# Five wider tiles of u, and weights made as (1 + fraction) times a power of two, in an attention and gated-FFN kernel that TensorE bounds

## The chip, the cores and the metric

The kernel runs on one core of one Trainium2 chip. The metric is the device time of one execution in microseconds (us). The engines are called PE (TensorE), DVE (VectorE), ACT (ScalarE), POOL (GpSimd) and SP (SyncE, which here issues transfers). All runs that are compared were in the fast state, at a mean granted PE clock of 0.997 to 1.0; a kernel that ran only once in a batch carries no state ("unknown"), and is used for its trace (and, for the changed kernel, as one of its 13 starts below). "Span" is the time from the first to the last instruction; the device time is 2.1 to 2.6 us longer. In the lines of the profile, PEld is the weight loads of PE, SPq the issuing of transfers, "L397" line 397 of the kernel, "at<-kv,qT" what is written and what is read, x12 a count, and a bracket at the end the idle time before the line and what ended it. Edits move the line numbers: the matmuls of the plain blocks are L397 in the kernel before, L400 in the changed one, L403 with the tiles alone and L394 with the conversion alone.

## The reference

Per batch and head (8 x 8, 576 tokens, 64 columns): `kv = k^T v`, `u = q kv`, and `x = u / rms(u) * g`. Then `out = (sigmoid(x Wg) * (x Wv)) Wo` on 4608 tokens, with 512 model columns and 1536 hidden columns.

```python
kv = np.einsum('bhsd,bhse->bhde', k, v)
out = np.einsum('bhsd,bhde->bhse', q, kv)
rms = np.sqrt(np.mean(out * out, axis=-1, keepdims=True) + 1e-06)
x = out / rms * g_norm
gate = 1.0 / (1.0 + np.exp(-(x @ w_gate)))
return gate * (x @ w_val) @ w_out
```

The three weights lie in HBM as 64-bit floats. The kernel has no such type, so it reads each as two 32-bit words and makes the 32-bit float by integer and float operations on 1024 columns a partition: one such group is a "unit", and there are 18 of them.

## The kernel before

Two heads are one "pair"; there are 32. The first eight go through a start of their own, in stages of several pairs at once; the other 24 are fed, piece by piece, between the matmuls of the FFN. u of a pair is made in six matmuls of 96 tokens:

```python
def u_mm():
    ps = at_ps("u")
    d["u"] = ps[0:NP, :, 0:JH * P]                    # NP = 96 tokens, P = 128 columns
    for j in range(NJ):                               # NJ = 6
        nc.tensor.matmul(ps[0:NP, j // JH, c0:c0 + P], d["qT"][...96 columns...], kvs[n % 2], ...)
```

The conversion of a unit is seven DVE steps (s0 to s6), and an Abs on ACT. The steps are handed out a few at a time, in the stages of the start and in the blocks of the first FFN layer ("plain" blocks, 16 matmul passes or 6.87 us of PE each):

```python
for i in range(NE + 1):                               # NE = 8 pairs
    stage(i, 3 if i < 2 else 1 if i == 2 else 0)      # second argument: conversion steps
    ...
blk = Plain(0, 0, ...)                                # block 0, chunk 0, weights of unit 0
for m in range(NMT): blk.mm(0, m)
do(NE - 1, U_SUM, U_ROOT)
take_abs(1)
do(NE - 2, X, X_OUT)
do(NE - 1, U_NORM)
convert_some(2)
... two matmuls, do(NE - 1, X, X_OUT), two matmuls ...
convert_some(2)
blk.gate()                                            # sigmoid on ACT
blk.end()                                             # gate product on DVE
blocks = [(1, 0)] + [(c, f) for f in range(1, NFT - 3) for c in range(2)] + ...
```

So unit 1 is first wanted by the third block, (0, 1).

Of the kernel before, what the change touches and what calls it, by code (L numbers as in the profile page):

```python
# [3 lines left out]

# [5 lines left out]

FP32 = mybir.dt.float32
U32 = mybir.dt.uint32
I64 = mybir.dt.int64
AF = mybir.ActivationFunctionType
ALU = mybir.AluOpType
AX = mybir.AxisListType


HI_MIN = struct.unpack("<f", struct.pack("<I", 0x38100000))[0]
HI_MAX = struct.unpack("<f", struct.pack("<I", 0x47EFFFFF))[0]  # L20


@with_exitstack
def kernel(
# [11 lines left out]
    nc = tc.nc  # L36

    B, H, S, HD = q.shape
    T, DM = out.shape
    DF = moe_w_gate.shape[1]  # L40
    P = 128
    NHP = H // 2
    NJ = 6
    NP = S // NJ
    JH = NJ // 2
    NMT = DM // P
    NFT = DF // P
    G = 512
# [41 lines left out]
    units = [("gv", f) for f in range(NFT)] + [("wo", f) for f in range(0, NFT, 2)]  # L90
    UW = 2 * NMT * P
    assert NMT * P == DM
    staged, absolute, w = {}, {}, {}

    def load_unit(u):
        if u >= len(units):
# [13 lines left out]
    def words(u):  # L110
        t = staged[u].rearrange("p i f -> p (i f)").bitcast(U32).rearrange("p (n two) -> p n two", two=2)
        return t[:, :, 0], t[:, :, 1]

    def take_abs(u):
        if u >= len(units):
            return
        absolute[u] = z = raw.tile([P, UW], U32, tag="cz", name="cz", bufs=2)
        nc.scalar.activation(out=z.bitcast(FP32), in_=words(u)[1].bitcast(FP32), func=AF.Abs)

    def convert(u):  # L120
        kind, f = units[u]
        vec = nc.vector
        d = {}

        def fl(t):
            return t.bitcast(FP32)

        def s0():

            t = const.tile([P, 2, DM], FP32, name=f"{kind}{f}") if kind == "gv" else w2[:, f:f + 2, :]  # L130
            if kind == "gv":
                for i, name in enumerate(("wg", "wv")):
                    w[name, f] = t[:, i].rearrange("p (m f) -> p m f", m=NMT)
            else:
                for i in range(2):
                    w["wo", f + i] = t[:, i]
            d["x"] = t.rearrange("p i f -> p (i f)").bitcast(U32)
            vec.tensor_scalar(out=fl(d["x"]), in0=fl(words(u)[1]), scalar1=HI_MAX, scalar2=-HI_MAX,
                              op0=ALU.min, op1=ALU.max)

        def s1():

            x, z = d["x"], absolute[u]
            vec.scalar_tensor_tensor(out=fl(x), in0=fl(z), scalar=HI_MIN, in1=fl(x), op0=ALU.is_ge, op1=ALU.mult)

        def s2():
            if u:
                take_abs(u + 1)

            vec.tensor_scalar(out=absolute[u], in0=d["x"], scalar1=0x07FFFFFF, scalar2=3, op0=ALU.bitwise_and,  # L150
                              op1=ALU.logical_shift_left)

        def s3():
            x, z = d["x"], absolute[u]
            vec.scalar_tensor_tensor(out=x, in0=x, scalar=0xC0000000, in1=z, op0=ALU.bitwise_and, op1=ALU.bitwise_or)

        def s4():

            vec.tensor_scalar(out=absolute[u], in0=d["x"], scalar1=0xFF800000, scalar2=None, op0=ALU.bitwise_and)

        def s5():
            z = absolute[u]
            vec.scalar_tensor_tensor(out=fl(z), in0=words(u)[0], scalar=2.0 ** -52, in1=fl(z),
                                     op0=ALU.mult, op1=ALU.mult)

        def s6():
            x, z = d["x"], absolute[u]
            vec.tensor_tensor(out=fl(x), in0=fl(z), in1=fl(x), op=ALU.add)
            if u:
                load_next_unit()  # L170

        return [s0, s1, s2, s3, s4, s5, s6]

    converts = deque(s for u in range(len(units)) for s in convert(u))
    made = [0]

    def convert_some(n):
        for _ in range(min(n, len(converts))):
            converts.popleft()()
            made[0] += 1  # L180

    def converted(u):
        convert_some(7 * (u + 1) - made[0])

    for n in range(4):
        load_kv(n)
# [26 lines left out]
    def attention(n, at_ps):  # L213

        b, m = divmod(n, NHP)
        d = {}

        def kv_mm():
            d["kv"] = ps = at_ps("kv")
            for j in range(NJ):  # L220
                js = slice(HD * j, HD * j + HD)
                for e in range(2):
                    nc.tensor.matmul(ps[HD * e:HD * e + HD, 0, 0:HD], pairs[n]["k"][:, e, js], pairs[n]["v"][:, e, js],  # L223
                                     start=(j == 0), stop=(j == NJ - 1))

        def kv_out():
            for e in range(2):
                es = slice(HD * e, HD * e + HD)
                nc.vector.tensor_copy(out=kvs[n % 2][es, es], in_=d["kv"][es, 0, 0:HD])
            for i in ahead(n, 2):  # L230
                load_kv(i)

        def q_mm():
            d["q"] = ps = at_ps("q")
            for j in range(NJ):
                c0 = NP * (j % JH)
                nc.tensor.transpose(ps[:, j // JH, c0:c0 + NP], pairs[n]["q"][:, j].rearrange("p e d -> p (e d)"),  # L237
                                    ident[0:NP, 0:NP])

        def q_out():  # L240
            d["qT"] = sb.tile([P, 2, JH * NP], FP32, tag="qT", name="qT")
            nc.scalar.copy(out=d["qT"], in_=d["q"][:, :, 0:JH * NP])
            for i in ahead(n, 1):
                load_q(i)

        def u_mm():

            ps = at_ps("u")
            d["u"] = ps[0:NP, :, 0:JH * P]
            for j in range(NJ):  # L250
                c0 = P * (j % JH)
                nc.tensor.matmul(ps[0:NP, j // JH, c0:c0 + P], d["qT"][:, j // JH, NP * (j % JH):NP * (j % JH) + NP],  # L252
                                 kvs[n % 2], start=True, stop=True)

        def u_square():
            d["sq"] = sb.tile([NP, 2, JH * P], FP32, tag="sq", name="sq")
            nc.scalar.activation(out=d["sq"], in_=d["u"], func=AF.Square)

        def u_sum():
            d["ms"] = sb.tile([NP, 2, 2 * JH], FP32, tag="ms", name="ms")  # L260
            nc.vector.tensor_reduce(out=d["ms"].rearrange("p i n -> p (i n)"),  # L261
                                    in_=d["sq"].rearrange("p i (n d) -> p (i n) d", d=HD), axis=AX.X, op=ALU.add)

        def u_root():
            nc.scalar.activation(out=d["ms"], in_=d["ms"], func=AF.Sqrt, bias=eps[0:NP], scale=1.0 / HD)

        def u_norm():
            nc.vector.reciprocal(d["ms"], d["ms"])
            d["xn"] = d["sq"]
            nc.vector.tensor_tensor(out=d["xn"].rearrange("p i (n d) -> p i n d", d=HD),  # L270
                                    in0=d["u"].rearrange("p i (n d) -> p i n d", d=HD),
                                    in1=d["ms"].unsqueeze(3).to_broadcast([NP, 2, 2 * JH, HD]), op=ALU.mult)

        def x_mm():
            d["x"] = ps = at_ps("x")
            for j in range(NJ):
                c0 = NP * (j % JH)
                nc.tensor.transpose(ps[:, j // JH, c0:c0 + NP], d["xn"][:, j // JH, P * (j % JH):P * (j % JH) + P],  # L278
                                    ident[0:NP, 0:NP])

        def x_out():

            s0 = 0
            while s0 < S:
                c, o = divmod(S * b + s0, G)
                i, r = divmod(s0, S // 2)
                n_ = min(G - o, S // 2 - r)
                nc.scalar.activation(out=chunk(c)[:, m, o:o + n_], in_=d["x"][:, i, r:r + n_], func=AF.Copy, scale=g_col)
                s0 += n_

        return [kv_mm, kv_out, q_mm, q_out, u_mm, u_square, u_sum, u_root, u_norm, x_mm, x_out]


# [119 lines left out]
    def halves(t):  # L413
        return t[:, 0], t[:, 1]
# [23 lines left out]
    def stage(i, n_convert):  # L438
        do(i, KV, Q, KV_OUT, Q_OUT)
        do(i - 2, U_SUM, U_ROOT, U_NORM)  # L440
        do(i - 1, U, U_SQUARE)
        do(i - 3, X, X_OUT)
        if i == 0:
            take_abs(0)
        convert_some(n_convert)

    for i in range(NE + 1):
        stage(i, 3 if i < 2 else 1 if i == 2 else 0)
        if i + 5 == NE:
            load_next_unit()  # L450
            load_next_unit()
# [1 line left out]
    for m in range(NMT):  # L453
        blk.mm(0, m)
    do(NE - 1, U_SUM, U_ROOT)
    take_abs(1)
    do(NE - 2, X, X_OUT)
    do(NE - 1, U_NORM)
    convert_some(2)
# [9 lines left out]
    blk.end()  # L469
    blocks = [(1, 0)] + [(c, f) for f in range(1, NFT - 3) for c in range(2)] + [(0, f) for f in range(NFT - 3, NFT)]  # L470
    for n, (c, f) in enumerate(blocks):
        plain(c, f, 7 if n == 0 else 6, halves(two(n % 4)))
    assert n % 4 == 3
    finish()
    convert_some(len(converts))
# [223 lines left out]
```

## Time and profile before

| before | us |
|---|---|
| device time, median of the first 3 runs | 1135.58 (1133.63 to 1135.91) |
| span of the profiled run | 1133.9 |
| PE busy | 1113.2 |
| first matmul of the first block | 45.82 |
| last matmul over | 1130.02 |
| rest (last sum, last store) | 3.88 |

The prediction shows the lines that carry this. For the argument, the span is cut in three: the **start**, up to the first matmul of the first block; the **stretch**, from there to the end of the last matmul, in which PE is fed almost without a gap; and the **rest**, after it. The stretch is 1130.02 - 45.82 = 1084.20 us.

### The profile page before, as it was taken

The page shows a single profiled execution, that of the slowest core. Times are in us where ns is not written, and L with a number is a line of the kernel's source. Part 1 is how long each engine was busy: PE and PEld are TensorE (multiplying, and loading weights), DVE is VectorE, ACT ScalarE, POOL GpSimd, SP SyncE. Part 2 cuts the span into 40 slices and gives each one's busy share as a digit, 9 for nine tenths or more (in the row PEclk, how much of TensorE's full clock was granted, in tenths as well). Part 3 has the DMA queues.
Part 4 walks back from the last instruction along what each step waited for, and adds up shares of the span by engine and source line. Part 5 has one row for each costly group of instructions (what it writes and reads, how often), then busy time and mean ns, then how long its engine had stood idle before and what let it go on. Part 6 is the DMA issues. An engine that isn't in the chain of part 4 may idle for free.

```text
span 1133.9 us, 14824 instructions
## 1 busy us (share of the span) xinstructions
PE 1113.2 (98%) x5712; PEld 892.0 (79%) x5712; DVE 582.1 (51%) x1121; ACT 296.9 (26%) x571; POOL 239.5 (21%) x342
## 2 busy tenths in 40 slices
PE   5899999999999999999999999999999999999998
PEld 5644444547888888888888888888888888888887
DVE  4699996054155624563365415552556246615641
ACT  3622221223033303331243213340333112101110
POOL 0000001000033303430133104330333035404420
PEclk9999999999999999999999999999999999999999
DMA  9943431220312012110202030201100000000001
GB/s 221 231 137 123 149 111 33 49 71 11 78 23 53 11 26 64 40 35 20 71 11 54 20 75 16 53 11 38 53 11 11 20 19 1 1 21 17 1 1 38
DMA packets 71589, 57.58 MB, mean 51 GB/s; under 512 B 40800, under 2 KB 65376, under 8 KB 71520
## 3 DMA queue, kind: packets, MB, share of 16 engines
q1 hardware_dynamic: 71360, 56.64, 19.3%
q8 instruction: 46, 0.75, 0.3%
q14 instruction: 23, 0.19, 0.1%
q10 hardware_dynamic: 160, 0.00, 0.0%
HBM read 47.19 MB, written 9.44 MB: 50 GB/s over the span
## 4 chain that ended last, share of the span: by engine, by line
PE 94%; DMA 3%; DVE 2%; SPq 0%; issue 0%; ACT 0%; DVEq 0%
PE mm L526 45%; PE mm L606 26%; PE two L397 10%; PE mm L382 4%; PE at L397 3%; DMA q<-in_q_dram 3%; PE at L252 3%; PE at L223 2%; PE at L278 1%; PE at L237 1%; PE mm L397 1%; DVE sq L270 0%; DVE ms L261 0%; SPq L85 0%; SPq L76 0%; DVE w L648 0%
## 5 line engine op out<-in xcount | busy, mean ns | idle before, releaser
L512 POOL TENSOR_TENSOR tw<-gv 128x256 f32<-128x256 f32 x168 | 120.4, 727 | 843.5 <-PE mm L526 653.7
L526 PE MATMUL mm<-xT,tw 128*128 128x256 f32 x672 | 159.7, 380 | 0.0
L526 PE MATMUL mm<-sx,tw 128*128 128x256 f32 x672 | 159.7, 380 | 0.0
L526 PE MATMUL mm<-xT,gv 128*128 128x256 f32 x672 | 158.8, 379 | 0.0
L526 PEld LDWEIGHTS mm<-xT,gv 128*128 128x128 f32 x672 | 127.7, 190 | 17.4
L526 PEld LDWEIGHTS mm<-sx,tw 128*128 128x128 f32 x672 | 126.1, 190 | 16.7
L526 PEld LDWEIGHTS mm<-xT,tw 128*128 128x128 f32 x672 | 125.3, 190 | 16.1
L512 POOL TENSOR_TENSOR tw<-gv,tw 128x256 f32<-128x256 f32 x168 | 123.6, 757 | 0.0
L397 PE MATMUL two<-xT,gv 128*128 128x512 f32 x256 | 111.1, 593 | 0.5 <-DVE sq L270 0.5
L397 PEld LDWEIGHTS two<-xT,gv 128*128 128x128 f32 x256 | 48.4, 190 | 60.4 <-issue 60.2
L606 PE MATMUL mm<-t2w,gv 128*128 128x256 f32 x384 | 89.1, 379 | 0.0
L606 PE MATMUL mm<-w,gv 128*128 128x256 f32 x384 | 88.1, 379 | 0.0
L606 PE MATMUL mm<-w,s 128*128 128x256 f32 x384 | 88.1, 379 | 0.0
L555 ACT ACTIVATE sg<-sg 128x256 f32<-128x256 f32 x84 | 35.0, 417 | 190.2 <-DVE sg L554 188.9
L546 DVE TENSOR_TENSOR gv<-mm,sg 128x256 f32<-128x256 f32 x84 | 35.7, 425 | 88.5 <-PE mm L526 88.5
L606 PEld LDWEIGHTS mm<-w,s 128*128 128x128 f32 x384 | 73.0, 190 | 9.9
L606 PEld LDWEIGHTS mm<-t2w,gv 128*128 128x128 f32 x384 | 72.6, 190 | 9.7
L606 PEld LDWEIGHTS mm<-w,gv 128*128 128x128 f32 x384 | 72.5, 190 | 9.6
L526 PE MATMUL mm<-sx,gv 128*128 128x256 f32 x336 | 79.5, 379 | 0.0
L526 PEld LDWEIGHTS mm<-sx,gv 128*128 128x128 f32 x336 | 63.1, 190 | 8.2
L533 ACT COPY sg<-mm 128x256 f32<-128x256 f32 x84 | 31.3, 373 | 140.6 <-PE mm L526 140.4
L562 DVE TENSOR_TENSOR gv<-gv,sg 128x512 f32<-128x512 f32 x84 | 67.1, 838 | 0.2
(94 smaller groups left out, 1191.1 us busy)
## 6 DMA issues: line engine op xcount, KB each, us to landing
k<-in_k_dram SPq DMA_DIRECT2D x32, 288.0 KB, 4.8
v<-in_v_dram SPq DMA_DIRECT2D x32, 288.0 KB, 5.3
q<-in_q_dram SPq DMA_DIRECT2D x64, 144.0 KB, 3.2
st<-in_moe_w_gate_dram SPq DMA_DIRECT2D x12, 512.0 KB, 3.7
st<-in_moe_w_val_dram SPq DMA_DIRECT2D x12, 512.0 KB, 4.7
st<-in_moe_w_out_dram SPq DMA_DIRECT2D x12, 512.0 KB, 4.4
out_dram<-sg SPq DMA_DIRECT2D x24, 192.0 KB, 2.2
out_dram<-sg SPq DMA_DIRECT2D x24, 128.0 KB, 2.3
```

The lines of the kernel that those rows point to most:

```text
L223: nc.tensor.matmul(ps[HD * e:HD * e + HD, 0, 0:HD], pairs[n]["k"][:, e, js], pairs[n]["v"][:, e, js], start=(j == 0), stop=(j == NJ - 1))
L237: nc.tensor.transpose(ps[:, j // JH, c0:c0 + NP], pairs[n]["q"][:, j].rearrange("p e d -> p (e d)"), ident[0:NP, 0:NP])
L252: nc.tensor.matmul(ps[0:NP, j // JH, c0:c0 + P], d["qT"][:, j // JH, NP * (j % JH):NP * (j % JH) + NP], kvs[n % 2], start=True, stop=True)
L382: nc.tensor.matmul(ps, gv[c, f][:, P * t:P * t + P], w["wo", f], start=(f == 0), stop=(f == NFT - 1))
L397: nc.tensor.matmul(self.ps[i], w[("wg", "wv")[i], self.f][:, m, :], xT[self.c][:, m, :], start=(m == 0), stop=(m == NMT - 1), skip_group_c ...
L512: nc.gpsimd.tensor_tensor(out=tw[f, i], in0=b[in0], in1=b[in1] if isinstance(in1, tuple) else tw[f, in1], op=ALU.subtract)
L526: nc.tensor.matmul(ps, wt[:, m, :], xs[:, m, :], start=(new and m == 0), stop=(m == NK - 1), skip_group_check=True)
L533: nc.scalar.copy(out=d["sg"][:, h2], in_=pa)
L546: tt(out=d["h"][:, h2], in0=pb, in1=d["sg"][:, h2], op=ALU.add)
L555: nc.scalar.activation(out=d["sg"][:, h2], in_=d["sg"][:, h2], func=AF.Sigmoid)
L562: tt(out=d["h"], in0=d["h"], in1=d["sg"], op=ALU.mult)
L606: nc.tensor.matmul(ps, hs(f), ws[:, f, :], start=(new and f == 0), stop=(f == NF2 - 1), skip_group_check=True)
```

## The change

Its intent: fewer passes on PE for u, and less DVE work for the weights. u gets five tiles of 115 tokens, each read as 116 rows. A weight is made as m = 1 + fraction (mask on DVE, scale and add on ACT), a power of two p (shift on DVE, integer arithmetic on ACT), then low word, sign and product in three two-source steps on DVE. The first two steps of a unit run one unit ahead, so that ACT has time.

```diff
+    NU = 5
+    M = S // NU
+    MU = S - M * (NU - 1)
+    UC = 192
...  (u_mm)
-            for j in range(NJ):
-                nc.tensor.matmul(ps[0:NP, ...], d["qT"][...], kvs[n % 2], start=True, stop=True)
+            for i in range(NU):
+                nc.tensor.matmul(d["u"][:, i], qT[:, M * i:M * i + MU], kvs[n % 2], start=True, stop=True)
...  (square, sum, normalisation: 96 x 768 becomes 116 x 640; transposes of x: five of 115 or 116)
...  (convert: the seven steps become five)
+            vec.tensor_scalar(out=m.bitcast(U32), in0=words(u)[1], scalar1=0x000FFFFF, ..., op0=ALU.bitwise_and)
+            nc.scalar.activation(out=m, in_=m.bitcast(U32), func=AF.Identity, scale=2.0 ** -20, bias=one)
+            vec.tensor_scalar(out=p, in0=words(u)[1], scalar1=20, scalar2=0x7FF, ...)
+            nc.scalar.activation(out=p.bitcast(I32), in_=p, func=AF.Relu, scale=2.0 ** 23, bias=exp_off)
+            vec.scalar_tensor_tensor(out=m, in0=words(u)[0], scalar=2.0 ** -52, in1=m, op0=ALU.mult, op1=ALU.add)
+            vec.scalar_tensor_tensor(out=p, in0=words(u)[1], scalar=0x80000000, in1=p, ...)
+            vec.tensor_tensor(out=m, in0=m, in1=d["p"].bitcast(FP32), op=ALU.mult)
...
+    converts.extend(halves_of[0][0] + halves_of[0][1] + halves_of[1][0])
+    last[0] = 5
+    for u in range(1, len(units)):
+        if u + 1 < len(units):
+            converts.extend(halves_of[u + 1][0])
+        converts.extend(halves_of[u][1])
+        last[u] = len(converts)
...
-        stage(i, 3 if i < 2 else 1 if i == 2 else 0)
+        stage(i, 2 if i < 2 else 1 if i == 2 else 0)
...
-        plain(c, f, 7 if n == 0 else 6, halves(two(n % 4)))
+        plain(c, f, 5, halves(two(n % 4)))
```

More of the change, by code (lines that the diff above doesn't have):

```diff
@@ L1 @@
-import struct
 from collections import deque
@@ L12 @@
 U32 = mybir.dt.uint32
+I32 = mybir.dt.int32
 I64 = mybir.dt.int64
@@ L16 @@
 AX = mybir.AxisListType
-HI_MIN = struct.unpack("<f", struct.pack("<I", 0x38100000))[0]
-HI_MAX = struct.unpack("<f", struct.pack("<I", 0x47EFFFFF))[0]
 @with_exitstack
@@ L45 @@
     JH = NJ // 2
+    NU = 5
+    M = S // NU
+    MU = S - M * (NU - 1)
+    UC = 192
+    UX = M * 3
     NMT = DM // P
@@ L92 @@
     assert NMT * P == DM
-    staged, absolute, w = {}, {}, {}
+    staged, w = {}, {}
     def load_unit(u):
@@ L112, in words @@
         return t[:, :, 0], t[:, :, 1]
-    def take_abs(u):
-        if u >= len(units):
-            return
-        absolute[u] = z = raw.tile([P, UW], U32, tag="cz", name="cz", bufs=2)
-        nc.scalar.activation(out=z.bitcast(FP32), in_=words(u)[1].bitcast(FP32), func=AF.Abs)
+    EXP_OFF = 896
+    one = const.tile([P, 1], FP32, name="one")
+    nc.vector.memset(one, 1.0)
+    exp_off = const.tile([P, 1], FP32, name="exp_off")
+    nc.vector.memset(exp_off, -EXP_OFF * 2.0 ** 23)
     def convert(u):
@@ L123, in convert @@
         d = {}
-        def fl(t):
-            return t.bitcast(FP32)
         def s0():
@@ L136, in s0 @@
                     w["wo", f + i] = t[:, i]
-            d["x"] = t.rearrange("p i f -> p (i f)").bitcast(U32)
-            vec.tensor_scalar(out=fl(d["x"]), in0=fl(words(u)[1]), scalar1=HI_MAX, scalar2=-HI_MAX,
-                              op0=ALU.min, op1=ALU.max)
+            d["m"] = m = t.rearrange("p i f -> p (i f)")
+            vec.tensor_scalar(out=m.bitcast(U32), in0=words(u)[1], scalar1=0x000FFFFF, scalar2=None,
+                              op0=ALU.bitwise_and)
+            nc.scalar.activation(out=m, in_=m.bitcast(U32), func=AF.Identity, scale=2.0 ** -20, bias=one)
@@ L141, in s1 @@
         def s1():
-            x, z = d["x"], absolute[u]
-            vec.scalar_tensor_tensor(out=fl(x), in0=fl(z), scalar=HI_MIN, in1=fl(x), op0=ALU.is_ge, op1=ALU.mult)
+            d["p"] = p = raw.tile([P, UW], U32, tag="cz", name="cz", bufs=2)
+            vec.tensor_scalar(out=p, in0=words(u)[1], scalar1=20, scalar2=0x7FF, op0=ALU.logical_shift_right,
+                              op1=ALU.bitwise_and)
+            nc.scalar.activation(out=p.bitcast(I32), in_=p, func=AF.Relu, scale=2.0 ** 23, bias=exp_off)
@@ L146, in s2 @@
         def s2():
-            if u:
-                take_abs(u + 1)
-            vec.tensor_scalar(out=absolute[u], in0=d["x"], scalar1=0x07FFFFFF, scalar2=3, op0=ALU.bitwise_and,
-                              op1=ALU.logical_shift_left)
+            m = d["m"]
+            vec.scalar_tensor_tensor(out=m, in0=words(u)[0], scalar=2.0 ** -52, in1=m, op0=ALU.mult, op1=ALU.add)
         def s3():
-            x, z = d["x"], absolute[u]
-            vec.scalar_tensor_tensor(out=x, in0=x, scalar=0xC0000000, in1=z, op0=ALU.bitwise_and, op1=ALU.bitwise_or)
+            p = d["p"]
@@ L157, in s4 @@
+            vec.scalar_tensor_tensor(out=p, in0=words(u)[1], scalar=0x80000000, in1=p, op0=ALU.bitwise_and,
+                                     op1=ALU.bitwise_or)
         def s4():
-            vec.tensor_scalar(out=absolute[u], in0=d["x"], scalar1=0xFF800000, scalar2=None, op0=ALU.bitwise_and)
-        def s5():
-            z = absolute[u]
-            vec.scalar_tensor_tensor(out=fl(z), in0=words(u)[0], scalar=2.0 ** -52, in1=fl(z),
-                                     op0=ALU.mult, op1=ALU.mult)
@@ L166, in s6 @@
-        def s6():
-            x, z = d["x"], absolute[u]
-            vec.tensor_tensor(out=fl(x), in0=fl(z), in1=fl(x), op=ALU.add)
+            m = d["m"]
+            vec.tensor_tensor(out=m, in0=m, in1=d["p"].bitcast(FP32), op=ALU.mult)
             if u:
                 load_next_unit()
-        return [s0, s1, s2, s3, s4, s5, s6]
-    converts = deque(s for u in range(len(units)) for s in convert(u))
+        return [s0, s1], [s2, s3, s4]
+    halves_of = [convert(u) for u in range(len(units))]
@@ L175 @@
+    converts, last = deque(), {}
+    converts.extend(halves_of[0][0] + halves_of[0][1] + halves_of[1][0])
[5 more added lines that the diff above has]
+        last[u] = len(converts)
     made = [0]
@@ L182, in converted @@
     def converted(u):
-        convert_some(7 * (u + 1) - made[0])
+        convert_some(last[u] - made[0])
     for n in range(4):
@@ L248, in u_mm @@
             ps = at_ps("u")
-            d["u"] = ps[0:NP, :, 0:JH * P]
-            for j in range(NJ):
-                c0 = P * (j % JH)
-                nc.tensor.matmul(ps[0:NP, j // JH, c0:c0 + P], d["qT"][:, j // JH, NP * (j % JH):NP * (j % JH) + NP],
-                                 kvs[n % 2], start=True, stop=True)
+            d["u"] = ps[0:MU].rearrange("p i c -> p (i c)")[:, 0:NU * UC].rearrange("p (i c) -> p i c", c=UC)[:, :, 0:P]
+            qT = d["qT"].rearrange("p i n -> p (i n)")
+            for i in range(NU):
+                nc.tensor.matmul(d["u"][:, i], qT[:, M * i:M * i + MU], kvs[n % 2], start=True, stop=True)
         def u_square():
-            d["sq"] = sb.tile([NP, 2, JH * P], FP32, tag="sq", name="sq")
+            d["sq"] = sb.tile([MU, NU, P], FP32, tag="sq", name="sq")
             nc.scalar.activation(out=d["sq"], in_=d["u"], func=AF.Square)
         def u_sum():
-            d["ms"] = sb.tile([NP, 2, 2 * JH], FP32, tag="ms", name="ms")
-            nc.vector.tensor_reduce(out=d["ms"].rearrange("p i n -> p (i n)"),
-                                    in_=d["sq"].rearrange("p i (n d) -> p (i n) d", d=HD), axis=AX.X, op=ALU.add)
+            d["ms"] = sb.tile([MU, NU, 2], FP32, tag="ms", name="ms")
+            nc.vector.tensor_reduce(out=d["ms"].rearrange("p i e -> p (i e)"),
+                                    in_=d["sq"].rearrange("p i (e d) -> p (i e) d", d=HD), axis=AX.X, op=ALU.add)
         def u_root():
-            nc.scalar.activation(out=d["ms"], in_=d["ms"], func=AF.Sqrt, bias=eps[0:NP], scale=1.0 / HD)
+            nc.scalar.activation(out=d["ms"], in_=d["ms"], func=AF.Sqrt, bias=eps[0:MU], scale=1.0 / HD)
         def u_norm():
@@ L269, in u_norm @@
             d["xn"] = d["sq"]
-            nc.vector.tensor_tensor(out=d["xn"].rearrange("p i (n d) -> p i n d", d=HD),
-                                    in0=d["u"].rearrange("p i (n d) -> p i n d", d=HD),
-                                    in1=d["ms"].unsqueeze(3).to_broadcast([NP, 2, 2 * JH, HD]), op=ALU.mult)
+            nc.vector.tensor_tensor(out=d["xn"].rearrange("p i (e d) -> p i e d", d=HD),
+                                    in0=d["u"].rearrange("p i (e d) -> p i e d", d=HD),
+                                    in1=d["ms"].unsqueeze(3).to_broadcast([MU, NU, 2, HD]), op=ALU.mult)
         def x_mm():
             d["x"] = ps = at_ps("x")
-            for j in range(NJ):
-                c0 = NP * (j % JH)
-                nc.tensor.transpose(ps[:, j // JH, c0:c0 + NP], d["xn"][:, j // JH, P * (j % JH):P * (j % JH) + P],
-                                    ident[0:NP, 0:NP])
+            for i in range(NU):
+                m_ = MU if i == NU - 1 else M
+                bank, c0 = divmod(M * i, UX)
+                nc.tensor.transpose(ps[:, bank, c0:c0 + m_], d["xn"][0:m_, i, :], ident[0:m_, 0:m_])
         def x_out():
@@ L285, in x_out @@
                 c, o = divmod(S * b + s0, G)
-                i, r = divmod(s0, S // 2)
-                n_ = min(G - o, S // 2 - r)
+                i, r = divmod(s0, UX)
+                n_ = min(G - o, (UX if i == 0 else S - UX) - r)
                 nc.scalar.activation(out=chunk(c)[:, m, o:o + n_], in_=d["x"][:, i, r:r + n_], func=AF.Copy, scale=g_col)
@@ L442, in stage @@
         do(i - 3, X, X_OUT)
-        if i == 0:
-            take_abs(0)
         convert_some(n_convert)
     for i in range(NE + 1):
-        stage(i, 3 if i < 2 else 1 if i == 2 else 0)
+        stage(i, 2 if i < 2 else 1 if i == 2 else 0)
         if i + 5 == NE:
@@ L455 @@
     do(NE - 1, U_SUM, U_ROOT)
-    take_abs(1)
     do(NE - 2, X, X_OUT)
```

## The prediction

> **What bounds the kernel now.** I read the page's busy shares and chain first, then the chain in order of time, then the timelines of the two places where TensorE (PE) is not the releaser.
>
> ```profile
> PE 1113.2 (98%) x5712; PEld 892.0 (79%) x5712; DVE 582.1 (51%) x1121; ACT 296.9 (26%) x571; POOL 239.5 (21%) x342
> ...
> PE 94%; DMA 3%; DVE 2%; SPq 0%; issue 0%; ACT 0%; DVEq 0%
> ```
>
> PE is busy 98% of the span and is 94% of the chain that ended last; VectorE (DVE), which the change mostly relieves, is busy for half of the span and is 2% of the chain. A busy share alone proves little, so I looked at what the PE waits for, in the list of waits cut to PE. After the first attention pairs it has one wait in the rest of the run, 1.3 us for a DVE normalisation; before that, waits for data and for the same DVE line:
>
> ```profile
> PE at L278 <- DVE sq L270: 1.3, 1, 1.3
> PE two L397 <- DVE sq L270: 0.5, 1, 0.5
> ```
>
> The window from 60 to 192 us, where all weights are converted on a DVE that is over 90% busy, has no PE wait at all. So four stretches count: a start of about 39.3 us that is paced by transfers (the chain there is one q load after another, 8.28, 8.27, 8.73 and 7.56 us long), a latency chain from 39.4 to 45.8 us, a PE that streams from 45.8 us to the end, and the one wait at 254.6 us. The chain in order of time, in the second stretch, with its start and its length:
>
> ```profile
> 40.62 0.96 DVE ms L261
> ...
> 41.61 0.32 ACT ms L265
> ...
> 42.20 0.95 DVE sq L270
> 43.16 0.87 DVE ms L261
> ...
> 44.72 0.97 DVE sq L270
> 45.68 0.14 issue
> 45.82 3.67 PE two L397 x8
> ...
> 52.23 22.34 PE two L397 x52
> ```
>
> Here the reader is to see that two sums (L261) and two normalisations (L270) of DVE lie on the path, and that from 45.82 us on matmuls follow each other. In the streaming stretch the u product of one pair (L252) sits between others; the timeline of PE gives its price by the start of what follows:
>
> ```profile
> 337.59 1.47 PE L252 MATMUL at<-kv,qT 128*96 128x128 f32 x12
> 338.90 1.89 PE L526 MATMUL mm<-xT,tw 128*128 128x256 f32 x8
> ```
>
> Twelve passes (each fp32 matmul is two) take 338.90 - 337.59 = 1.31 us of PE, 109.2 ns a pass, although one is recorded as 273 ns: the record is latency, the distance is cost. Eight passes of 256 columns are 1.73 us apart (216 ns), so the cost goes with the moving columns.
>
> **What the Trainium skill says.** "VectorE: DVE Perf Modes", section "The perf-mode tier table", has a one-source fp32 tensor_scalar at twice the rate of a two-source operation. The trace agrees: 1024 columns take 0.69 us in L138, L150 and L159, and 1.22 us in L144, L155, L163 and L168. "ScalarE: Activation LUTs", section "What ACT_TABLE_LOAD costs", gives an activation with a pointer bias 280 ns + 0.833 ns a column, so 1.13 us for 1024 columns, with some 93 ns of overlap back to back; L118 took 1.13 to 1.17 us here, so I use 1.13. Its section "Table sets: the hidden batching unit" puts relu, identity and abs in every set; the builds of both kernels indeed have 49 table loads each. "TensorE: Matmul & The Clock Gate", section "LDWEIGHTS", gives columns / 1.2 ns. The two weight loads of this trace, 190 ns at 128 columns and 163 at 96, differ by 0.84 ns a column, which agrees with the slope; an estimate of 97 ns at 116 columns stays under the 109 ns of the pass above it, so wider u tiles should not make the weight load the limit.
>
> **The change part by part.**
>
> Tiles of u. Six matmuls of 96 tokens become five of 115 or 116, each with 128 moving columns. Each pair loses two passes: 2 x 109.2 = 0.218 us. There are 32 pairs; eight lie in the start and the latency chain, 24 in the streaming stretch: 24 x 0.218 = 5.24 us, straight off the path. The transposes of x (L278) move the token columns, 6 x 96 = 576 before and 4 x 115 + 116 = 575 or 576 after, so their 0.50 us stays. The copies of x on ScalarE (ACT) are three per pair with the same sum of columns.
>
> Softer work per pair. The square on ACT, the sum and the normalisation on DVE go from 768 to 640 columns. DVE's rows are 0.95 us at 768; 128 columns at 1 column per 0.96 GHz cycle (1024 columns in 1.22 us less a fixed part) are 0.133 us. In the latency chain there are four such steps: 4 x 0.133 = 0.53 us earlier start of the stream. At the wait of 254.6 us the DVE chain becomes 0.27 us shorter and the PE arrives 0.22 us earlier, so the gain there is 0.05 us beyond the removed matmul.
>
> Conversion of weights. 18 units. Before, three one-source and four two-source steps: 3 x 0.69 + 4 x 1.22 = 6.95 us, and one Abs. After, two one-source (and, shift) and three two-source: 2 x 0.69 + 3 x 1.22 = 5.04 us, and two activations. DVE loses 18 x 1.9 = 34 us; ACT gains 18 x 1.13 = 20 us. In a block of 6.87 us of PE, DVE falls from about 6 x 0.99 + 0.6 = 6.6 to 5.04 + 0.6 = 5.7 us. Since the PE waits for none of it, I book nothing for this.
>
> Order at the first blocks. Here I found the only place where the change can cost. The weights of unit 1 are needed when the third block starts, at 52.23 us + 20 passes x 0.4296 = 60.82 us. Before, DVE does four of its seven steps ahead of the first gate product (L405), and three after:
>
> ```profile
> 54.34 1.28 ACT L402 ACT_TABLE_LOAD   x1
> ...
> 55.64 0.60 ACT L402 ACTIVATE sg<-two 128x512 f32<-128x512 f32 x1
> ...
> 56.27 0.69 DVE L405 TENSOR_TENSOR gv<-two,sg 128x512 f32<-128x512 f32 x1 [3.49 <-ACT sg L402]
> ...
> 56.88 0.68 DVE L159 TENSOR_SCALAR cz<-gv 128x1024 uint32<-128x1024 uint32 x1
> ...
> 57.59 1.23 DVE L163 SCALAR_TENSOR_TENSOR cz<-st,cz 128x1024 f32<-128x1024 uint32 x1
> ...
> 58.85 1.22 DVE L168 TENSOR_TENSOR gv<-cz,gv 128x1024 f32<-128x1024 f32 x1
> ```
>
> It ends at 60.07 us, only 0.75 us early. The order of instructions of the changed kernel shows the first halves of units 1 and 2 ahead of that product, but all three two-source steps of unit 1 behind it, and ACT with two activations for unit 2 where one Abs (53.19 us) stood ahead of the table load and the sigmoid. With everything 0.53 us earlier: ACT's two activations from 52.66, done 52.66 + 1.04 + 1.13 = 54.83; table load to 56.13; sigmoid to 56.75; gate product at 56.78, next step at 57.39; steps of 1.26, 1.26 and 1.22 us end at 61.13. The PE wants it at 60.82 - 0.53 = 60.29. Estimated new stall: 61.15 - 60.29 = 0.86 us, once. Later blocks run ahead: one unit per block is made, one per two blocks is used.
>
> Staging buffers. With one unit ahead, a buffer is read until the fourth step of its unit, so the load three units on has less room: about 1.2 + 1.4 + 3.7 + 0.6 us plus DVE's idle time of a block (1.2), some 8 us, before its first step. A unit is 1.05 MB in some 5 us at the 200 GB/s of the bursts there, so it fits; a late one would only eat into a lead of units.
>
> Sum: -5.24 - 0.53 - 0.05 + 0.86 = -4.96 us. 1135.58 - 4.96 = 1130.6 us.
>
> **The rivals.**
>
> First: DVE's 34 us come through, at least in the converting stretch of 140 us, giving 1100 us or so. For it speaks only that DVE is over 90% busy there. Against it: no PE wait between 60 and 192 us. I give it 1 in 100.
>
> Second: the wait moves to the new ACT work. A larger stall than computed, if the table load or the late second activation holds the first sigmoid, or repeated stalls if the staging loads come too late. It would make 1 to 3 us of loss in place of 0.86: 1131 to 1133 us. For it: the margin is already under 1 us. Against: from the fourth block on the lead grows.
>
> Third: the 116-column weight load, from starts 460 bytes apart instead of 384, or PSUM slots 192 columns apart, costs the u product its gain. If a pass became 131 ns, ten would take the old 1.31 us and the time would be 1135 to 1136. No row in this trace shows such a shape; the slope of the weight loads speaks against it.
>
> Fourth: the start gets shorter through less DVE work. The q loads set it; at most a few tenths.
>
> **Range and chances.** The certain part is a count, 5.2 us; the two start-up terms are each good to about half a microsecond; three runs of the kernel before spread over 2.3 us, which is the largest part of the range. So 1130.6 us, 1128.2 to 1132.8 eight times in ten. Two per cent would be 22.7 us: faster 0.01, within 2% 0.98, slower 0.01.
>
> **What would show it right or wrong.** L256 with 320 instead of 384 passes, and ten of them 1.09 us apart from the next matmul in the stream; if 1.31, the third rival. A PE wait of 0.5 to 1.5 us for the last conversion step (L163) near 60 us; none would make the time about 1129.7. The first block's matmuls starting near 45.3 instead of 45.8 us. DVE busy lower by some 34 us from conversion and about 9 from attention, ACT higher by some 16, with PE still over 98%. A time under 1125 would mean that I misjudged what the PE waits for; over 1134, a stall I didn't see.

## The result, and the profile after

The changed kernel took 1129.07 us (median of 6 runs, 1128.47 to 1130.14), against 1135.33 us (6 runs, 1133.63 to 1137.60). The ratio is 0.9946 (95% interval 0.9933 to 0.9959). A ratio here is the mean time of one kernel's fast runs over that of the other's in the same rounds, so it is not quite the ratio of the medians. It is within 2%, and inside the predicted range.

The busy shares and the chain of the page after the change:

```profile
PE 1106.3 (98%) x5616; PEld 884.9 (79%) x5616; DVE 536.6 (48%) x1087; ACT 310.5 (28%) x589; POOL 239.5 (21%) x342
...
PE 94%; DMA 2%; DVE 2%; ACT 1%; SPq 0%; issue 0%; DVEq 0%
```

PE has 96 passes less (three per pair: two of u, and one transpose) and is as busy as before. DVE lost 45 us and ACT gained 14. None of that says where 6 us come from. The cut in three does: the first block starts at 42.91 us, the last matmul is over at 1123.34 us, so

| us | before | after | difference | predicted |
|---|---|---|---|---|
| start | 45.82 | 42.91 | -2.91 | -0.53 |
| stretch | 1084.20 | 1080.43 | -3.77 | -4.43 |
| rest | 3.88 | 3.86 | -0.02 | 0 |

The total lay in the range, and both of its parts were off. First the u product, in the timeline of PE (start, length, engine, line, operation, shapes, count):

```profile
335.31 1.25 PE L256 MATMUL at<-kv,qT 128*116 128x128 f32 x10
336.40 1.89 PE L526 MATMUL mm<-xT,tw 128*128 128x256 f32 x8
```

Ten passes take 336.40 - 335.31 = 1.09 us of PE, where twelve took 1.31. This is what was predicted; the wider weight load (116 columns) slows nothing.

Then the third block. The timeline of PE has the first two blocks' remaining passes and the third block's first:

```profile
49.15 8.76 PE L400 MATMUL two<-xT,gv 128*128 128x512 f32 x20
59.55 6.68 PE L400 MATMUL two<-xT,gv 128*128 128x512 f32 x15 [1.65 <-DVE gv L163]
```

Twenty passes of 0.4293 us from 49.15 end at 57.74 us as PE counts them, and the next starts at 59.55: 1.81 us late (the profile says 1.65, since a pass's record is longer than its share of PE). The predicted wait is there, at the predicted place and for the predicted instruction, and twice as long. The chain of work over it shows why:

```profile
47.12 1.04 ACT xT L291 x3
48.16 1.04 ACT gv L141
49.20 1.03 ACT cz L149
50.24 0.94 ACT xT L291 x3
51.17 1.03 ACT gv L141
52.21 1.04 ACT cz L149
53.24 0.02 issue
53.26 1.28 ACT L405
...
54.55 0.61 ACT sg L405
...
55.18 0.69 DVE gv L408
55.88 1.13 DVE gv L154
57.01 1.15 DVE cz L158
...
58.18 1.24 DVE gv L163
59.41 0.14 issue
59.55 6.68 PE two L400 x15
```

ACT is the path without a gap from 47.12 to 55.18 us: copies of x, two activations of unit 1, copies of x, two activations of unit 2, a table load and the first sigmoid. Only then DVE does the gate product (L408) and the three last steps of unit 1, for which PE waits. In the kernel before, the timeline of ACT has gaps in the same place:

```profile
50.02 1.04 ACT L288 ACTIVATE xT<-two,g_col 128x288 f32<-128x288 f32 x3 [1.44 <-PE two L278]
52.27 1.04 ACT L288 ACTIVATE xT<-at,g_col 128x288 f32<-128x288 f32 x3 [1.20 <-PE at L278]
53.19 1.13 ACT L118 ACTIVATE cz<-st 128x1024 f32<-128x1024 f32 x1
```

The second gap, 1.20 us, is shorter than the two activations (2.07 us) that the change puts into it. My prediction counted unit 2's activations, which stand where one Abs stood, and forgot unit 1's.

### The profile page after: what moved, and what is told of

Its sections match the earlier page's. It is cut to its first block, busy times and chain, and to the rows that moved or that the text cites. A ratio compares the mean times of both kernels' runs of the same rounds, so it can differ in the third digit from the quotient of the medians.

```text
span 1127.2 us, 14586 instructions
## 1 busy us (share of the span) xinstructions
PE 1106.3 (98%) x5616; PEld 884.9 (79%) x5616; DVE 536.6 (48%) x1087; ACT 310.5 (28%) x589; POOL 239.5 (21%) x342
## 4 chain that ended last, share of the span: by engine, by line
PE 94%; DMA 2%; DVE 2%; ACT 1%; SPq 0%; issue 0%; DVEq 0%
PE mm L526 45%; PE mm L606 26%; PE two L400 9%; PE mm L385 4%; PE at L400 3%; PE at L256 2%; PE at L227 2%; DMA q<-in_q_dram 1%; PE at L241 1%; PE at L282 1%; PE mm L400 1%; DMA v<-in_v_dram 1%; PE two L256 0%; DVE sq L273 0%; DVE ms L264 0%; ACT gv L141 0%
```

## The experiments

All outputs are right. The stretch is read from the trace as above. The start of each timed run is its span less the stretch and less 3.87 us; this takes for granted that stretch and rest repeat, as they do in the traces.

**1. Both kernels again, one look each.** No edit.

> The kernel before, unchanged, for its trace. Open: the last q load of the start landed at 36.9 us in the changed kernel and 39.3 us in the kernel before, with the transfers at 246 to 250 GB/s against 220 to 226. Theory A (the rate of the transfers is the chance of a run): this trace need not show 220 to 226 GB/s between 12 and 36 us again; anything from 215 to 255 and a first matmul of the first block (L397) between 42.5 and 46.5 us. Theory B (the change makes the transfers faster): again 220 to 226 GB/s and 45.8 us within 0.3.

> The changed kernel, unchanged, for its trace. Theory A: a rate between 12 and 36 us that may well differ from 246 to 250 GB/s, first matmul of the first block anywhere from 42 to 46 us. Theory B: again 246 to 250 GB/s and 42.9 us within 0.3. Both: a wait of the PE for the last conversion step (L163) of 1.5 to 1.8 us.

The kernel before started at 45.07 us this time, the changed one at 43.33; the stretches were 1084.22 and 1080.43 us, 0.02 and 0.00 us from the first traces. The transfers between 12 and 36 us ran at 239 GB/s in the first and 246 in the second. Theory B fails, since neither start came back within 0.3 us, nor the rate of the kernel before. All values lie in the wide bands of theory A, so the 223 GB/s of the first trace were chance; but a start 1.7 us shorter stayed, and A gives no reason for it.

**2. The two halves of the change, each alone.** The diff split: the parts on `NU` and the u, square, sum, normalisation and transpose steps; and all the rest.

```diff
 u_only:    + five tiles of u, transposes of 115 or 116   (conversion as before)
 conv_only: + new conversion, one unit ahead              (u in six tiles of 96)
```

> Five tiles of u alone, with the old conversion. My theory: 10 passes of 109 ns in the u product, 24 pairs x 0.218 = 5.24 us off the stream, 0.5 us off the latency chain, no PE wait at the third block: 5.8 us less than before, ratio 0.9949, and the time from the first block's first matmul to the end 5.2 to 5.4 us shorter. Rival (the conversion is what gains, by a faster start): under 4 us. If the wider tiles also made the start's transfers faster (theory B with the tiles): 8 us less and over 240 GB/s from 12 to 36 us.

> The new conversion alone, with six tiles of u. My theory: the stream is longer by the new wait at the third block, 1.5 to 1.8 us, and nothing is gained: 1.3 to 1.8 us slower than before, ratio 1.0012 to 1.0016. Theory B with the conversion as the cause: the start is some 2.4 us shorter (over 240 GB/s from 12 to 36 us), so 0.6 to 0.9 us faster, ratio 0.9993.

Five tiles alone: 1129.33 us (ratio 0.9942, 0.9930 to 0.9955), stretch 1078.55 us, which is 5.66 less than before. The conversion alone: 1136.58 us (1.0007, 0.9993 to 1.0020), stretch 1086.03 us, 1.82 more. The sum, -3.84, is the change's -3.78 within 0.06 us. The time of the conversion alone fell between the two theories written for it (0.8 us more than before, where they had 1.3 to 1.8 more and 0.6 to 0.9 less), since its starts were shorter as well. The stretch is settled: **the tiles give all of the gain, the conversion gives nothing and costs one wait.** Busy times in 117 us of the converting blocks (columns: window, its length, busy us and instructions of PE, PEld, DVE, ACT, POOL, then clock, transfers' share, GB/s), in the first trace of the kernel before:

```profile
74.50:191.30 116.80, 116.80 (x274) 51.75 (x273) 106.72 (x116) 25.06 (x30) 5.51 (x8) 1.00 0.32 108
```

And in the trace of the conversion alone:

```profile
74.50:191.30 116.80, 116.80 (x274) 51.72 (x273) 77.37 (x87) 36.96 (x43) 5.51 (x8) 1.00 0.32 108
```

DVE fell from 106.72 to 77.37 us, and PE did the same 274 passes in the same time.

The tiles gave 0.37 us more in the stretch than the 5.29 predicted. Part of that is in the transposes, which I had booked as unchanged. Before, from transposes over the next group to the one after it:

```profile
329.63 0.66 PE L278 MATMUL at<-ident,sq 96*128 96x96 f32 x6
330.12 1.92 PE L526 MATMUL mm<-sx,gv 128*128 128x256 f32 x8
331.88 1.89 PE L526 MATMUL mm<-xT,gv 128*128 128x256 f32 x8
```

After:

```profile
327.37 0.66 PE L282 MATMUL at<-ident,sq 115*128 115x115 f32 x5
327.87 1.90 PE L526 MATMUL mm<-sx,gv 128*128 128x256 f32 x8
329.60 1.89 PE L526 MATMUL mm<-xT,gv 128*128 128x256 f32 x8
```

2.25 us became 2.23: not the transposes themselves but the group behind them starts up 0.03 us sooner. At 0.02 us a pair this is some 0.4 to 0.5 us for 24 pairs, which is the size of what was missing. It is not this one place: in the traces of the kernel before and of the tiles alone, the group behind the transposes is shorter by about 0.02 us at all 24 pairs (eight passes, for instance, 1.75 or 1.76 us before and 1.73 or 1.74 after), apart from those at which a matmul record is missing. Why it starts up sooner no run shows.

**3. Unit 1's activations moved into a gap.** The prediction's own figure of 0.86 us should come out when the forgotten work is taken off the path.

```diff
     do(NE - 1, U_SUM, U_ROOT)
+    convert_some(2)
     do(NE - 2, X, X_OUT)
     do(NE - 1, U_NORM)
-    convert_some(2)
```

> The changed kernel with the first half of unit 1 one step earlier, so that its two activations run in ScalarE's gap ahead of the x copies of the last but one pair. Measured in the changed kernel: the third block starts 1.81 us late (from the end of 20 passes of 0.4293 us to the next matmul). Theory: of this my prediction's 0.86 us are the two activations of unit 2, and the rest is those of unit 1, which I had not counted; so here 0.85 to 1.0 us late, and 1079.5 us from the first matmul of the first block to the last of the kernel in place of 1080.43. Rival (unit 1's activations cost nothing, the wait is the DVE steps or the table load being longer than computed): 1.8 us as before.

The timeline of PE:

```profile
49.98 8.76 PE L400 MATMUL two<-xT,gv 128*128 128x512 f32 x20
59.60 13.97 PE L400 MATMUL two<-xT,gv 128*128 128x512 f32 x32 [0.86 <-DVE gv L163]
```

The third block is 59.60 - (49.98 + 8.59) = 1.03 us late in place of 1.81, and the stretch is 1079.64 us, 0.79 less. So unit 1's two activations were 0.8 us of the wait, as the theory said, and the rival falls. The 1.03 are 0.03 over my band.

**4. Unit 1 finished ahead of the first gate product.** DVE idles there for 7.12 us in the changed kernel, in front of that product.

```diff
-    converts.extend(halves_of[0][0] + halves_of[0][1] + halves_of[1][0])
-    last[0] = 5
-    for u in range(1, len(units)):
+    converts.extend(halves_of[0][0] + halves_of[0][1] + halves_of[1][0] + halves_of[1][1] + halves_of[2][0])
+    last[0], last[1] = 5, 10
+    for u in range(2, len(units)):
...
-    convert_some(2)
+    convert_some(3)
     blk.gate()
```

> The changed kernel with unit 1 finished ahead of the first gate product and unit 2's first half behind it. Theory: no PE wait at the third block, 1078.5 to 1078.7 us from the first matmul of the first block to the last (as with five tiles alone, 1078.55), 1.8 us less than the changed kernel: 1127.2 us, ratio to before 0.993. Rival (the wait moves on to unit 2, two blocks later, or the staging loads come too late): a new PE wait of 0.5 us or more near 70 us.

In the timeline of PE the three blocks are now one piece, without a wait:

```profile
51.41 22.49 PE L400 MATMUL two<-xT,gv 128*128 128x512 f32 x52
```

The stretch is 1078.54 us, 1.89 less than the changed kernel and equal to that of the tiles alone. No new wait appears. Yet the time was 1129.01 us (4 runs, ratio 0.9941, 0.9926 to 0.9955), not the 1127.2 expected: its starts were 42.8, 43.8, 45.1 and 45.2 us. Up to that point its instructions, on every engine and on the transfer queue, are those of the changed kernel in the same order, whose starts average 42.7 us over 13 runs. So the mean starts of two kernels can differ by 1.5 us for no reason in their instructions (over 4 and 13 runs), and the time alone could not have shown the gain of this edit.

**5. The table loads out of the start.** A dummy square root, first thing on ACT, moves the load of its table to where ACT is idle.

```diff
     nc.vector.memset(eps, 1e-6)
+    warm = const.tile([P, 1], FP32, name="warm")
+    nc.scalar.activation(out=warm, in_=eps, func=AF.Sqrt)
```

> The kernel before with a dummy square root on ScalarE at its very start, so that the two table loads of 1.28 us leave the start's pairs. If the start is paced by the transfers alone (as the prediction had it): the first matmul of the first block at 45.0 to 45.8 us as before, no gain. If it is paced by the work of the pairs on PE, DVE and ScalarE as well, as the chains of the repeats suggest: 0.7 to 1.3 us earlier, 43.8 to 44.3 us, and the time 0.7 to 1.3 us less, ratio 0.9990.

> The changed kernel with the same dummy square root. Its chain in the start is loads (q and v) for most of the time, so both theories expect little: the first matmul at 42.7 to 43.3 us (42.91 and 43.33 without), under 0.5 us less time. If it gains over 1 us, then the work of the pairs paces this start too, in spite of what its chain shows.

On the kernel before: 1134.59 us (4 runs), ratio 1.0003 (0.9981 to 1.0024); the trace started at 42.85 us, but at 251 GB/s, and the timed starts range from 42.8 to 47.8 us. This is inconclusive: the chance of the start is larger than the effect asked for. On the changed kernel: 1129.59 us, ratio 0.9949 (0.9934 to 0.9964), starts of 43.3 us on the mean, which is no gain, as both theories had it.

**6. Everything again for the starts, and the best version.** The last kernel is experiment 4 and the dummy square root together.

> The changed kernel again, five timed rounds on the same chip as the two halves of the change. The stretch from the first matmul of the first block to the last matmul has repeated to 0.02 us for each kernel, so the span of each timed run less this stretch and 3.87 us at the end gives its start. So far: before 45.2 us (16 runs, 43.5 to 46.8), this kernel 42.6 (6 runs), tiles alone 44.5 (5), conversion alone 44.5 (5). Expected if the whole change's start is better than both halves by a real effect: a mean start of 42.5 to 43.1. If the first value was partly chance: 43.3 to 44.3, so a time of 1129.7 to 1130.7 us.

> Five tiles alone again. The stretch of PE 1078.55 us as before. Start: my theory (the pairs' own work on PE and DVE shares in the pacing wherever the transfers run near 245 GB/s, and the tiles shorten it) 43.5 to 44.5 us on the mean; rival (the start is the chance of the transfers alone): that of before on the same chip, within 0.5.

> The new conversion alone again. The stretch of PE 1086.03 us as before. Start: my theory 44.2 to 44.9 us on the mean, 0.3 to 1.0 less than before on the same chip; rival: that of before within 0.3. Time: 0.3 to 1.5 us more than before, ratio 1.0003 to 1.0013.

> The changed kernel with unit 1 finished ahead of the first gate product, and the dummy square root at the start. The stretch of PE 1078.54 us, 1.89 us under the changed kernel, and a start of 42.5 to 43.5 us on the mean: 1127.0 to 1128.0 us, 1.9 us (1.4 to 2.5) less than the changed kernel on the same chip. If the order gives back at the start what it gains at the third block, as the single runs so far would allow: the same time as the changed kernel within 0.5 us.

The stretches were again 1080.43, 1078.54, 1086.04 and 1078.56 us. Times: changed kernel 1128.95 us (ratio 0.9941), tiles alone 1129.65 (0.9950, 0.9935 to 0.9964), conversion alone 1135.95 (1.0005, 0.9990 to 1.0020), best 1128.37 (0.9936, 0.9922 to 0.9951). The best version beats the kernel before; its PE stretch is 1.87 us shorter than the changed kernel's, but its 0.6 us over that one lie within the spread, since its starts again came out higher (43.7 us on the mean). That is nearer the second expectation for it than the first.

The starts of this batch, against what was expected: the changed kernel's mean of 42.6 us is in the band of a real effect. The conversion alone came out at 44.1, 0.1 us under my theory's 44.2 to 44.9 and outside the rival's 0.3 us of before (45.0 on this chip). The tiles alone came out at 44.9: my theory (43.5 to 44.5) missed, and the rival's value (that of before within 0.5) came.

All starts, with the mean transfer rates between 12 and 36 us of the profiled runs:

| kernel | timed runs | mean start, us | lowest, highest | rates in traces, GB/s |
|---|---|---|---|---|
| before | 18 | 45.1 | 43.5, 46.8 | 223, 239 |
| conversion alone | 9 | 44.3 | 43.7, 44.8 | 245, 249 |
| tiles alone | 9 | 44.6 | 43.0, 45.6 | 241, 242 |
| changed | 13 | 42.7 | 41.6, 43.7 | 248, 246, 238 |
| unit 1 finished early | 4 | 44.2 | 42.8, 45.2 | 229 |
| best | 5 | 43.7 | 42.0, 45.0 | 252 |

What sets the start? The prediction said the loads of q. In some traces that is so, as in both of the tiles alone. The end of the chain in the first of them, from its last load of q:

```profile
29.53 7.92 DMA q<-in_q_dram
...
37.59 0.70 PE at L244 x6
...
43.45 3.67 PE two L403 x8
```

In others it is not. The chain of the conversion alone leaves the loads at 12.66 us and never comes back to them:

```profile
5.08 7.59 DMA v<-in_v_dram
...
12.80 1.55 PE at L220 x24
...
21.47 1.28 ACT L262
...
28.43 1.55 PE two L249 x12
29.98 0.50 PE two L275 x6
30.48 0.85 PE at L220 x24
31.32 0.65 PE at L234 x6
31.97 1.31 PE two L249 x12
...
37.97 0.66 PE at L234 x6
...
44.34 3.67 PE two L394 x8
```

Here the pairs' own work is the path: a table load, then PE with u, x, kv and q of one pair after the other (1.31 + 0.50 + 0.85 + 0.65 = 3.3 us a pair), then the DVE chain. Its starts are also the narrowest of the four kernels with nine runs or more, 43.7 to 44.8 us. So two paths lie close together in the start: transfers, whose rate differs from run to run, and the work of the pairs. That the start is the later of the two, and that the change helps by shortening the second, is what I take from the chains; no run shows it by itself, and the tiles alone speak against it. Their start is 0.5 us less than before, and that is no more than what follows the last transposes of q: 43.45 - 37.59 = 5.86 us here, 6.41 in the kernel before (and 44.34 - 37.97 = 6.37 with the conversion alone).

The rate goes with the start as well. In the seven traces of kernels with both halves of the change, the first matmul comes at 45.18 us at 229 GB/s, at 43.33 to 43.75 at 238 to 246, at 42.91 at 248 and at 42.02 at 252. Near 240 GB/s the kernel before started at 45.07, the tiles alone at 43.45 and 44.57. Which of rate and start is the cause isn't shown, since loads also wait for buffers that the work of the pairs frees (in the changed kernel, those of q for 0.7 us on transposes of x and 0.4 us on the u product).

## Why the prediction was right or wrong

- **The total.** 1130.6 us predicted, 1129.07 measured, range 1128.2 to 1132.8. The mechanism, passes of PE taken off a stream, was right. Three terms were mis-sized, and their errors partly cancel: the tiles gave 0.4 us and the start 1.9 us more than booked, the wait took 1.0 us more. That the total came within 1.6 us is in part luck.
- **Tiles of u, -5.24 us.** Right in kind, and its unit price exact: 1.31 to 1.09 us a pair. The whole term was -5.66 in the stretch, with the 0.05 of the wait at 254 us in it. "So their 0.50 us stays" was right for the transposes and left out the group behind them.
- **The weight load at 116 columns.** Right: the u passes stay 109 ns apart, and the load's record went from 163 to 180 ns, 0.85 ns a column.
- **DVE's 34 us booked as nothing.** Right, and shown by the conversion alone: 29 us less DVE in those 117 us (37 in the whole run), and the same PE.
- **The wait at the third block, +0.86 us.** Right place, right instruction, and mis-sized: 1.81 us (1.65 in the profile's own count, over the 0.5 to 1.5 that I had named as the sign). The step that failed is "ACT's two activations from 52.66". It took the start of the x copies from before, but those had to wait for two activations of unit 1 that the prediction's own listing of the order contains. Experiment 3 priced them at 0.79 us. In the trace unit 2's activations start 8.26 us after the first block (51.17 - 42.91), where the prediction had 7.37 (52.66 - 45.29). The rest of the miss is small slips: the third block was taken as due from the chain, which has the matmuls from 52.23 us, where the timeline of PE has 52.06 (0.17 us); the 0.14 us between DVE's end and PE's start in the chains were left out; and some steps were 0.25 us shorter in sum than booked. The recorded sum itself ends at 61.13 us, not at the 61.15 that it then uses, and L118's activations took up to 1.19 us, not 1.17.
- **"Staging buffers" and the second rival.** No wait of PE came from later units or loads. The rival's form of a longer first wait was what happened.
- **The latency chain, -0.53 us.** Right: from the last transposes of q to the first block 45.82 - 39.41 = 6.41 us before, 42.91 - 37.05 = 5.86 after, -0.55.
- **"A start of about 39.3 us that is paced by transfers", and the fourth rival's "at most a few tenths".** This is what failed most: the start became 2.4 us shorter on the mean (45.1 to 42.7) and 0.53 had been booked. The step was to read one trace of before, with slow transfers and loads as the path throughout, as what always paces the start. Repeats show the pairs' work in the chain too. The change takes 0.22 us of PE and some 0.26 us of DVE from each pair, and two DVE steps from the first stages; that this is what shortens the start is a guess that no run confirms.
- **What stays open.** The cause of the shorter start, beyond the 0.55 us of the latency chain. The halves alone gave 0.5 and 0.8 us and the whole 2.4. That surplus of 1.1 us is smaller than the 1.5 us by which experiment 4 differs from the changed kernel with the same instructions. Over all 27 runs of kernels with both halves the mean start is 43.2 us, 1.9 less than before. I can't say which part of it is the change. The device time also exceeds the span by 2.1 to 2.2 us in every run with the new conversion and by 2.1 to 2.6 in the others; some 0.3 us of the gain are there, for a cause that no run showed.

## What to carry to other kernels

Where PE is fed without a gap, count the passes removed from it first: here 10 passes for 12 gave the gain of the stretch (but for some 0.4 us behind the transposes), and over a quarter of DVE's work in the converting blocks gave none. When work moves from one engine to another, walk through the order of the engine that gets it, instruction by instruction, at the first place where its result is wanted, and count every piece that now stands ahead of it, also those that seem to fall in a gap. And cut the span into a part that repeats and a part that doesn't before comparing: a difference of 1.9 us was exact to 0.02 in the stretch and invisible in the times.

## What the Trainium skill lacked or had wrong

- "ScalarE: Activation LUTs", section "What ACT_TABLE_LOAD costs": its price of an activation agrees. It lacks a word on integer operands; activations of 1024 columns from unsigned 32-bit words to float or to signed 32-bit words took 1.14 to 1.15 us on the mean here and 1.04 back to back, as the page has it for floats. Its table load, 1.28 us here too, stood on the path by itself in front of the first sigmoid, without the further 1.38 us of drain that the section adds: the activation before it ended 0.02 us earlier, and the sigmoid started 0.01 us after it.
- "TensorE: Matmul & The Clock Gate", section "LDWEIGHTS": the slope agrees (0.84 and 0.85 ns a column between 96, 128 and 116 columns). That page lacks the price of 32-bit matmuls in a stream: here a matmul is two passes, each 109 ns for 128 columns and 216 ns for 256. It gives transposes by their duration, not by their cost in a stream: six 96-column transposes took 0.49 us of PE between other matmuls, though one is recorded as 246 ns, and the group behind them started up to 0.03 us later than behind five of 115.
- No page that I read has how much the rate of the same loads differs from run to run: 223 to 252 GB/s between 12 and 36 us in fourteen traces whose kernels issue the same loads in the same order, and starts that spread over 3.3 us for one kernel.
